# Epsilon as a third triple of the variance, and a reordered first chunk, in a fused attention and gated-unit kernel

## The chip, the cores and the metric

The kernel runs on one core of a Trainium2 chip. The metric is device time in microseconds, the median over several executions. In the traces the core's engines are PE (TensorE; PEld is its weight loads), DVE (VectorE), ACT (ScalarE), POOL (GpSimd) and SP (SyncE, which here only issues DMAs). All times below are microseconds unless marked otherwise, and "L193" is line 193 of the kernel before the change.

## What is computed

Two branches read the same layer-normed input and are added to the input itself:

```python
xn = layernorm(x, eps=1e-5)                      # x: 2048 rows of 512, bf16
# A: attention, 32 heads of 16, each row sees itself and the 255 rows before it
q, k, v = split(xn @ wqkv)                       # wqkv: 512 x 1536
p = softmax(mask(q k^T / 4, window 256))
a = (p v) @ wo                                   # wo: 512 x 512
# B: bilinear gated unit
b = ((xn @ w_gate) * (xn @ w_up)) @ w_down       # 512 x 1792, 512 x 1792, 1792 x 512
out = x + a + b
```

The layer norm has neither scale nor shift: each row is `(x - mean) * (var + 1e-5) ** -0.5`.

## The kernel before

The 2048 rows are cut into 16 blocks of 128 rows, and four blocks make a chunk T of 512 rows, so there are four chunks. All weights are loaded once, by DMAs that SP issues at the start: x of blocks 0, 1 and 2 to 3 first, then the three thirds of Wqkv (V, K, Q), then halves of the gate and up weights, the rest of x and the other weights.

The order of instructions on every engine is written out by hand. `run` walks through a list of attention steps and, between them, takes pieces of other matrix work (projections of the next chunk, gate, up and down products) from the list that `fillers` makes, by a running count of PE time; each engine then executes its own instructions in that order and waits on semaphores for the others. `copy` picks ACT or DVE for an eviction by booked time, unless the caller names the engine. `PADS` puts 298 empty PE instructions (nops, L682) into two later stretches.

What matters here is how a block is normed, and the start.

For block t, `norm_stats` (L187) runs two DVE instructions: `bn_stats` (L193) turns the 512 values of a row into two triples of count, mean and sum of squares (6 numbers), and `bn_aggr` (L194) joins the triples into a mean and a variance (`mv`). `norm_scale` (L198) adds 1e-5 to the variance (`ve`, L203: on DVE for block 0, on POOL for all others) and takes the power -0.5 on POOL (`rs`, L206). `norm_apply` (L210) writes `xn = (x - mean) * rs` on DVE (L214). The tile `xn` has two buffers. `norm_transpose` (L219) turns a block by four PE transposes into a bank of PSUM (`xTp`, L233), which ACT copies to `xnT` (L234); from chunk 1 on, a DMA does this instead (L227).

PSUM has eight banks. Four of them ("M" banks) are taken in turn by `m_tile`; the other four make the score tile S, which the first attention step fills. `usual_banks(3)` starts the turn at bank 3.

The start goes like this on PE. `setup` first writes a zero tile and calls `keep_busy(40)`: 40 matmuls of 128 columns on that tile (`wps`, L151), whose result nobody reads. Then `first_chunk` (L292) follows. On DVE it puts the stats of blocks 0 and 1, then xn of block 0, the stats of block 2, xn of block 1, the stats of block 3, and xn of block 2. On PE it puts the transposes of block 0, `keep_busy(8)`, and then, for each block b from 0 to 3, the transposes of block b + 1 followed by the four matmuls of V of block b (`proj_v`, `vp`, L263). The copy of a V block from PSUM (L256 on DVE, L254 on ACT for block 2) is issued right behind its matmuls, and xn of block 3 is issued on DVE behind the copy of V0:

```python
for b in range(4):
    if b < 3:
        self.norm_transpose(b + 1, False)
    self.proj_v(b, engine="act" if b == 2 else "dve")
    if b == 0:
        self.norm_apply(3)
```

The K and Q projections of the chunk (`qkp`, L275) come next, and then the attention steps with their fillers. The norms of later chunks run among the fillers, in the same functions.

Of the kernel before, what the change touches and what calls it, by code (L numbers as in the profile page):

```python
# [8 lines left out]
F32 = mybir.dt.float32  # L9
I32 = mybir.dt.int32  # L10
ACT = mybir.ActivationFunctionType
ALU = mybir.AluOpType
# [24 lines left out]
class Kernel:  # L37
    def __init__(self, ctx, tc, x, wqkv, wo, wg, wu, wd, out):
        self.ctx, self.tc, self.nc = ctx, tc, tc.nc
        _, S, D = x.shape  # L40
        self.S, self.D, self.F = S, D, wg.shape[1]
        assert D == 512 and S % 512 == 0 and self.F % 256 == 0
        self.NT, self.NCH, self.NF = S // 128, S // 512, self.F // 128
        self.x_d, self.out_d = x.flatten_outer_dims(), out.flatten_outer_dims()
        self.w_d = dict(qkv=wqkv, o=wo, g=wg, u=wu, d=wd)

        def pool(name, bufs, **kw):
            return ctx.enter_context(tc.tile_pool(name=name, bufs=bufs, **kw))

        self.const = pool("const", 1)  # L50
        self.chunk2 = pool("chunk2", 2)
        self.qpool = pool("qpool", 5)
        self.kpool = pool("kpool", 9)
        self.hpool = pool("hpool", self.NF + FIRST)
        self.ppool = pool("ppool", 11)
        self.work = pool("work", 2)
        self.small = pool("small", 4)
        self.work1 = pool("work1", 1)
        self.psum = []
        self.usual_banks(3)  # L60

    def open_banks(self, name, bufs=1):

# [18 lines left out]
    def setup(self):  # L82
        nc, const, NT, NF = self.nc, self.const, self.NT, self.NF
        self.x = const.tile([128, NT, 512], BF16, name="x")
        self.Wqkv = const.tile([128, 4, 1536], BF16, name="Wqkv")
        self.Wo = const.tile([128, 4, 512], BF16, name="Wo")
        self.Wg = const.tile([128, 4, self.F], BF16, name="Wg")
        self.Wu = const.tile([128, 4, self.F], BF16, name="Wu")
        self.Wd = const.tile([128, NF, 512], BF16, name="Wd")
        xv = self.x_d.rearrange("(t p) d -> p t d", p=128)  # L90
        wq = self.w_d["qkv"].rearrange("(k p) n -> p k n", p=128)
        wg = self.w_d["g"].rearrange("(k p) n -> p k n", p=128)
        wu = self.w_d["u"].rearrange("(k p) n -> p k n", p=128)
        for lo, hi in ((0, 1), (1, 2), (2, 4)):
            nc.sync.dma_start(out=self.x[:, lo:hi, :], in_=xv[:, lo:hi, :])
        for lo in (1024, 512, 0):
            nc.sync.dma_start(out=self.Wqkv[:, :, lo:lo + 512], in_=wq[:, :, lo:lo + 512])
        h = self.F // 2
        for lo in (0, h):
            nc.sync.dma_start(out=self.Wg[:, :, lo:lo + h], in_=wg[:, :, lo:lo + h])  # L100
            nc.sync.dma_start(out=self.Wu[:, :, lo:lo + h], in_=wu[:, :, lo:lo + h])
            if lo == 0:
                nc.sync.dma_start(out=self.x[:, 4:8, :], in_=xv[:, 4:8, :])
        nc.sync.dma_start(out=self.Wd[:], in_=self.w_d["d"].rearrange("(f p) n -> p f n", p=128))
        wo = self.w_d["o"].rearrange("(c p) n -> p c n", p=128)
        for c in range(4):
            nc.sync.dma_start(out=self.Wo[:, c, :], in_=wo[:, c, :])
        for lo, hi in ((8, 10), (10, 12), (12, NT)):
            nc.sync.dma_start(out=self.x[:, lo:hi, :], in_=xv[:, lo:hi, :])

        self.idle = const.tile([128, 128], BF16, name="idle")
        nc.vector.memset(self.idle[:], 0.0)
        self.keep_busy(40)
        warm = const.tile([128, 1], F32, name="warm")
        nc.vector.memset(warm[:], 0.0)
        nc.scalar.activation(out=warm[:], in_=warm[:], func=ACT.Exp)
        ident = const.tile([128, 128], BF16, name="ident")
        nc.gpsimd.memset(ident[:], 0.0)
        nc.gpsimd.affine_select(out=ident[:], in_=ident[:], compare_op=ALU.not_equal, fill=1.0,
                                base=0, pattern=[[-1, 128]], channel_multiplier=1)  # L120
        self.ident = ident
        pi = const.tile([128, 1], I32, name="pi")
        nc.gpsimd.iota(pi[:], pattern=[[0, 1]], base=0, channel_multiplier=1)
        podd = const.tile([128, 1], I32, name="podd")
        nc.vector.tensor_scalar(out=podd[:], in0=pi[:], scalar1=4, scalar2=1,
                                op0=ALU.arith_shift_right, op1=ALU.bitwise_and)
        self.odd = const.tile([128, 1], F32, name="odd")
        nc.vector.tensor_copy(out=self.odd[:], in_=podd[:])
        self.even = const.tile([128, 1], F32, name="even")
        nc.vector.tensor_scalar(out=self.even[:], in0=self.odd[:], scalar1=-1.0, scalar2=1.0,  # L130
                                op0=ALU.mult, op1=ALU.add)
        self.mhalf = const.tile([128, 4], F32, name="mhalf")
        nc.gpsimd.memset(self.mhalf[:], -0.5)
        self.diag = const.tile([128, 64], BF16, name="diag")
        self.far = const.tile([128, 64], BF16, name="far")
        nc.gpsimd.memset(self.diag[:], BIG)
        nc.gpsimd.memset(self.far[:], BIG)
        for half in (slice(0, 64), slice(64, 128)):
            self.triangle(self.diag[half], True)
            self.triangle(self.far[half], False)  # L140
        self.xnT, self.Q, self.hT, self.OT = {}, {}, {}, {}
        self.K, self.V, self.VS = {}, {}, {}
        self.strips, self.parts, self.at = {}, {}, {}
        self.stock = []
        self.new_values()
# [41 lines left out]
    def norm_stats(self, t, n=4):  # L187

        nc = self.nc
        if t % n == 0:  # L190
            self.mv = self.small.tile([128, n, 2], F32, tag="mv", name="mv")
        st = self.small.tile([128, 6], F32, tag="st")
        nc.vector.bn_stats(out=st[:], in_=self.x[:, t, :])  # L193
        nc.vector.bn_aggr(out=self.mv[:, t % n, :], in_=st[:])  # L194
        self.book("dve", STATS)
        self.stats[t] = [self.mv, t % n, None]

    def norm_scale(self, t, n=4):  # L198

        nc = self.nc  # L200
        mv = self.stats[t][0]
        ve = self.small.tile([128, n], F32, tag="ve", name="ve")
        (nc.gpsimd if t else nc.vector).tensor_scalar(out=ve[:], in0=mv[:, :, 1], scalar1=1e-5, scalar2=None,  # L203
                                                      op0=ALU.add)
        rs = self.small.tile([128, n], F32, tag="rs", name="rs")
        nc.gpsimd.tensor_tensor(out=rs[:], in0=ve[:], in1=self.mhalf[:, 0:n], op=ALU.pow)  # L206
        for u in range(t, t + n):
            self.stats[u][2] = rs

# [45 lines left out]
        else:  # L255
            nc.vector.tensor_copy(out=out, in_=in_)  # L256

    def proj_v(self, t, ks=range(4), engine=None):
        nc = self.nc
        T, b = divmod(t, 4)  # L260
        ps = self.bank(ks, "vp")
        for k in ks:
            nc.tensor.matmul(ps[:], lhsT=self.xnT[T][:, b, k, :],  # L263
                             rhs=self.Wqkv[:, k, 1024:1536], start=(k == 0), stop=(k == 3))
        if 3 not in ks:
            return
        self.copy(self.heads(self.V[T])[:, b].rearrange("p (r g) d -> p r g d", r=2)[:, :, :, 0:16],
                  ps.rearrange("p (g r d) -> p r g d", g=16, r=2), engine)
# [23 lines left out]
    def first_chunk(self):  # L292

        self.new_chunk(0)
        for b in range(2):
            self.norm_stats(b, 1)
            self.norm_scale(b, 1)
        for b in (0, 1, 2):
            self.norm_apply(b)
            if b < 2:  # L300
                self.norm_stats(b + 2, 1)
                self.norm_scale(b + 2, 1)
        self.norm_transpose(0, False)
        self.keep_busy(8)
        for b in range(4):
            if b < 3:
                self.norm_transpose(b + 1, False)
            self.proj_v(b, engine="act" if b == 2 else "dve")
            if b == 0:
                self.norm_apply(3)  # L310
        self.proj_qk(0, 0, 1, engine="dve")
        self.proj_qk(0, 0, 0, engine="act")
        self.swap_halves(0, self.nc.scalar)
        self.proj_qk(0, 1, 1, engine="dve")
# [491 lines left out]
```

## Time and profile before

| | |
|---|---|
| median of 3 runs | 262.12 (262.10 to 262.45) |
| the profiled execution's own time | 262.46 |
| its span, from first to last instruction | 260.6 |
| instructions with a duration | 7774 |
| DMA traffic | 9.70 MB read, 2.10 MB written |

The span is what the profile's views cover; 1.86 of the profiled run lies around it. The profile's busy time of PE counts matmuls whose ends are modelled, so a busy PE may still have waited; only starts are measured. The granted clock of TensorE is 1.00 in every slice of the page. The most numerous group on POOL is the masking of attention probabilities (L182, 224 instructions, 98.7 busy), and on ACT the exponentials (L353, 66 of one form, 123.8 busy). The DMA engines are full from about 2 to 32, while the weights arrive.

In a line of the timeline, the columns are start, time from the first start to the last end, engine, line, operation, output and inputs, shapes and the number of instructions that the line merges; in brackets stands how long the engine had been idle before and what ended that.

### The profile page before, as it was taken

Reading aid. Unit: us, or ns where it says so; the run is one execution under the profiler, and the core shown is the slowest. Engines: PE = TensorE matmul, PEld = TensorE weight load, DVE = VectorE, ACT = ScalarE, POOL = GpSimd, SP = SyncE. Lnnn points to the kernel's source line nnn. Section 1 sums busy time; section 2 is a strip of 40 time slices with the busy share of each in tenths; the row PEclk is TensorE's granted clock in tenths of the full one; section 3 lists DMA queues with packets and bytes.
Section 4 is the critical chain, followed back from the end, with each engine's and each line's share of the span. In section 5 each row is a group of like instructions: output and inputs, shape, how many; then the busy total and the mean of one; then the engine's idle time right before and its main releaser. Section 6 shows DMA issues by size and latency. Waiting matters only on the chain.

```text
span 260.6 us, 7774 instructions
## 1 busy us (share of the span) xinstructions
PE 256.4 (98%) x3170; PEld 120.1 (46%) x3170; DVE 169.0 (65%) x342; ACT 183.4 (70%) x167; POOL 114.7 (44%) x278
## 2 busy tenths in 40 slices
PE   8999999999999999999999999999999999999995
PEld 8444444444444544444544454444544445444453
DVE  6687898888836487347976468642895235948144
ACT  3377788888586788787756768879874877877500
POOL 6216242425356745343445764334242565543500
DMA  6999910120013220002001301000200100000002
GB/s 207 377 353 336 283 27 20 24 48 1 3 40 43 60 25 1 3 0 48 3 3 41 82 24 23 0 4 1 48 5 4 36 23 24 3 0 3 3 0 83
DMA packets 19426, 15.04 MB, mean 58 GB/s; under 512 B 7360, under 2 KB 19392, under 8 KB 19392
## 3 DMA queue, kind: packets, MB, share of 16 engines
q1 hardware_dynamic: 18848, 14.26, 19.7%
q8 instruction: 26, 0.43, 0.7%
q10 hardware_dynamic: 544, 0.30, 0.4%
q14 instruction: 8, 0.07, 0.1%
HBM read 9.70 MB, written 2.10 MB: 45 GB/s over the span
## 4 chain that ended last, share of the span: by engine, by line
PE 91%; DVE 7%; issue 1%
PE up L513 17%; PE gp L502 17%; PE psd L535 16%; PE qkp L275 10%; PE S L350 8%; PE acc L473 6%; PE vp L263 6%; PE psd L541 5%; PE L L535 2%; PE wps L151 2%; DVE at L479 2%; DVE hT L518 1%; DVE on L492 1%; PE B L350 1%; PE L L541 1%
## 5 line engine op out<-in xcount | busy, mean ns | idle before, releaser
L182 POOL TENSOR_SCALAR_AFFINE_SELECT P<-P 64x256 bf16<-64x256 bf16 x224 | 98.7, 441 | 122.4 <-ACT P L353 110.7
L353 ACT ACTIVATE P<-S 128x2048 bf16<-128x2048 f32 x66 | 123.8, 1876 | 23.3 <-PE S L350 22.4
L502 PE MATMUL gp<-xnT,Wg 128*128 128x512 bf16 x224 | 59.1, 380 | 0.0
L513 PE MATMUL up<-xnT,Wu 128*128 128x512 bf16 x224 | 59.0, 380 | 0.0
L518 DVE TENSOR_TENSOR hT<-up,gsb 128x512 bf16<-128x512 f32 x56 | 38.0, 683 | 24.7 <-ACT gsb L254 12.7
L535 PE MATMUL psd<-Wd,hT 128*128 128x512 bf16 (+1 forms) x210 | 47.8, 369 | 0.0
L448 DVE TENSOR_TENSOR P<-P,diag 128x512 bf16<-128x512 bf16 (+1 forms) x75 | 30.1, 401 | 16.0 <-ACT P L353 15.9
L254 ACT ACTIVATE gsb<-gp 128x512 bf16<-128x512 f32 x49 | 28.5, 596 | 9.5 <-PE gp L502 9.4
L535 PEld LDWEIGHTS <-hT 128*128 128x128 bf16 x238 | 21.6, 98 | 25.5 <-issue 3.1
L513 PEld LDWEIGHTS <-Wu 128*128 128x128 bf16 x224 | 20.6, 98 | 25.6 <-issue 2.7
L502 PEld LDWEIGHTS <-Wg 128*128 128x128 bf16 x224 | 20.5, 98 | 25.5 <-issue 2.9
L353 ACT ACTIVATE P<-B 128x1536 bf16<-128x1536 f32 (+2 forms) x18 | 17.8, 1022 | 17.7 <-PE B L350 10.8
L275 PE MATMUL qkp<-xnT,Wqkv 128*128 128x512 bf16 x128 | 29.8, 380 | 0.0
L350 PE MATMUL S<-Q,K 32*128 32x320 bf16 (+4 forms) x624 | 28.7, 255 | 0.0
L350 PEld LDWEIGHTS <-K 32*128 32x128 bf16 x720 | 11.4, 92 | 27.4 <-issue 26.5
L551 DVE TENSOR_TENSOR x<-psd,x 128x512 bf16<-128x512 f32 (+1 forms) x15 | 9.9, 665 | 20.8 <-PE psd L541 20.8
L479 DVE STREAM_TRANSPOSE at<-acc 128x512 f32<-128x512 f32 x30 | 19.1, 688 | 4.6 <-PE acc L473 4.6
L275 PEld LDWEIGHTS <-Wqkv 128*128 128x128 bf16 x128 | 11.8, 98 | 14.7 <-issue 1.6
L473 PE MATMUL acc<-P,VS 64*32 64x320 bf16 (+4 forms) x672 | 17.6, 253 | 0.0
L473 PE MATMUL acc<-P,V 64*32 64x320 bf16 (+4 forms) x672 | 17.2, 253 | 0.0
L473 PEld LDWEIGHTS <-VS 64*32 64x32 bf16 x720 | 15.4, 91 | 2.2 <-issue 1.5
L263 PE MATMUL vp<-Wqkv,xnT 128*128 128x512 bf16 x64 | 15.3, 380 | 0.0
(56 smaller groups left out, 191.3 us busy)
## 6 DMA issues: line engine op xcount, KB each, us to landing
out_dram<-x SPq DMA_DIRECT2D x15, 128.0 KB, 1.7
Wg<-in_B_w_gate_dram SPq DMA_DIRECT2D x2, 896.0 KB, 11.3
Wu<-in_B_w_up_dram SPq DMA_DIRECT2D x2, 896.0 KB, 12.4
Wd<-in_B_w_down_dram SPq DMA_DIRECT2D x1, 1792.0 KB, 16.7
Wqkv<-in_A_wqkv_dram SPq DMA_DIRECT2D x3, 512.0 KB, 6.3
x<-in_A_x_dram SPq DMA_DIRECT2D x2, 512.0 KB, 8.8
VS<-V SPq DMA_DIRECT2D x6, 144.0 KB, 2.6
x<-in_A_x_dram SPq DMA_DIRECT2D x3, 256.0 KB, 6.7
```

Source lines behind the costliest of these rows:

```text
L182: nc.gpsimd.affine_select(out=v, in_=v, pattern=pattern + [[1 if diag else -1, 64]], compare_op=ALU.is_ge if diag else ALU.is_gt, fill=0.0 ...
L254: nc.scalar.activation(out=out, in_=in_, func=ACT.Copy)
L263: nc.tensor.matmul(ps[:], lhsT=self.xnT[T][:, b, k, :], rhs=self.Wqkv[:, k, 1024:1536], start=(k == 0), stop=(k == 3))
L275: nc.tensor.matmul(ps[:], lhsT=self.Wqkv[:, k, lo:lo + 128], rhs=self.xnT[T][:, :, k, :], start=(k == 0), stop=(k == 3))
L350: self.nc.tensor.matmul(kw.pop("out"), start=True, stop=True, skip_group_check=True, **kw)
L353: self.nc.scalar.activation(out=out, in_=in_, func=ACT.Exp, scale=0.25)
L448: self.nc.vector.tensor_tensor(out=v, in0=v, op=ALU.min, in1=self.diag.unsqueeze(1).unsqueeze(1).to_broadcast([128, 4, n, 64]))
L473: nc.tensor.matmul(accs[par][32 * e:32 * e + 32, q:q + n], lhsT=v, rhs=P[rows, e, col:col + n], start=(i == 0), stop=(i == len(todo) - 1), ...
L502: nc.tensor.matmul(ps[:], lhsT=self.Wg[:, k, 128 * f:128 * f + 128], rhs=self.xnT[T][:, :, k, :], start=(k == 0), stop=(k == 3))
L513: nc.tensor.matmul(ps[:], lhsT=self.Wu[:, k, 128 * f:128 * f + 128], rhs=self.xnT[T][:, :, k, :], start=(k == 0), stop=(k == 3))
L518: nc.vector.tensor_tensor(out=self.hT[T, f][:], in0=ps[:], in1=self.gsb[:], op=ALU.mult)
L535: nc.tensor.matmul(ps, lhsT=self.hT[T, f][:, 128 * b:128 * b + 128], rhs=self.Wd[:, f, c0:c1], start=(f == 0), stop=False)
```

## The change

There are five edits.

1. The statistics of a block go to a slice of a fixed tile `st` of 4 x 9 values instead of a fresh one of 6. The last three values of each slice are written once, by two POOL memsets in `setup`: count 0, mean 0, and a sum of squares of 512e-5. `bn_aggr` reads all nine, so that the variance comes out with 1e-5 in it. The addition `ve` is gone for all 16 blocks, and the power reads the variance directly.
2. The idle matmuls are 36 and 6 instead of 40 and 8.
3. xn of block 3 is issued on DVE ahead of V0's copy instead of behind it.
4. V0 is summed in the first bank of the score tile S instead of in an M bank. The turn of the M banks starts at 0 instead of 3, so that with one tile fewer taken from it every later tile has the bank that it had.
5. 4, 4 and 5 nops follow the matmuls of V1, V2 and V3 on PE.

```diff
-        self.usual_banks(3)
+        self.usual_banks(0)
...
-        self.keep_busy(40)
+        self.keep_busy(36)
...
+        self.st = const.tile([128, 4, 9], F32, name="st")
+        nc.gpsimd.memset(self.st[:, :, 6:8], 0.0)
+        nc.gpsimd.memset(self.st[:, :, 8:9], 512 * 1e-5)
         self.mhalf = const.tile([128, 4], F32, name="mhalf")
...
-        st = self.small.tile([128, 6], F32, tag="st")
-        nc.vector.bn_stats(out=st[:], in_=self.x[:, t, :])
-        nc.vector.bn_aggr(out=self.mv[:, t % n, :], in_=st[:])
+        st = self.st[:, t % 4, :]
+        nc.vector.bn_stats(out=st[:, 0:6], in_=self.x[:, t, :])
+        nc.vector.bn_aggr(out=self.mv[:, t % n, :], in_=st)
...
-        ve = self.small.tile([128, n], F32, tag="ve", name="ve")
-        (nc.gpsimd if t else nc.vector).tensor_scalar(out=ve[:], in0=mv[:, :, 1], scalar1=1e-5, scalar2=None,
-                                                      op0=ALU.add)
         rs = self.small.tile([128, n], F32, tag="rs", name="rs")
-        nc.gpsimd.tensor_tensor(out=rs[:], in0=ve[:], in1=self.mhalf[:, 0:n], op=ALU.pow)
+        nc.gpsimd.tensor_tensor(out=rs[:], in0=mv[:, :, 1], in1=self.mhalf[:, 0:n], op=ALU.pow)
...
-    def proj_v(self, t, ks=range(4), engine=None):
+    def proj_v(self, t, ks=range(4), engine=None, ps=None):
...
-        ps = self.bank(ks, "vp")
+        if ps is None:
+            ps = self.bank(ks, "vp")
...
         self.norm_transpose(0, False)
-        self.keep_busy(8)
+        self.keep_busy(6)
+        self.norm_apply(3)
+        S = self.s_tiles.tile([128, 4, 512], F32, tag="S", name="S")
         for b in range(4):
             if b < 3:
                 self.norm_transpose(b + 1, False)
-            self.proj_v(b, engine="act" if b == 2 else "dve")
-            if b == 0:
-                self.norm_apply(3)
+            self.proj_v(b, engine="act" if b == 2 else "dve", ps=None if b else S[:, 0, :])
+            for _ in range((0, 4, 4, 5)[b]):
+                self.nc.tensor.nop("pad", nofuse=True)
```

## The prediction

> **What bounds the kernel now.** I read the page first, then the timeline from 3 to 14 us engine by engine, because the diff acts there, and last every place where TensorE (PE) stands still. On the page:
>
> ```profile
> PE 256.4 (98%) x3170; PEld 120.1 (46%) x3170; DVE 169.0 (65%) x342; ACT 183.4 (70%) x167; POOL 114.7 (44%) x278
> ...
> PE 91%; DVE 7%; issue 1%
> ```
>
> The chain that ended last is PE nearly throughout, and POOL and ACT are not in it. So time can only come from PE being given less to do or from PE standing still less. PE's timeline at the start:
>
> ```profile
> 5.30 0.62 PE L233 MATMUL xTp<-ident,xn 128*128 128x128 bf16 x4
> 5.71 1.06 PE L151 MATMUL wps<-idle 128*128 128x128 bf16 x8
> 6.56 0.59 PE L233 MATMUL xTp<-ident,xn 128*128 128x128 bf16 x4
> 6.98 1.03 PE L263 MATMUL vp<-Wqkv,xnT 128*128 128x512 bf16 x4
> 7.85 0.39 PE L233 MATMUL xTp<-ident,xn 128*128 128x128 bf16 x4
> 8.07 1.03 PE L263 MATMUL vp<-Wqkv,xnT 128*128 128x512 bf16 x4
> 9.12 0.40 PE L233 MATMUL xTp<-ident,xn 128*128 128x128 bf16 x4
> ```
>
> Only the starts are used here, since the ends are modelled. Two things are to be seen. First, PE's pace doubles: eight idle matmuls take 6.56 - 5.71 = 0.85, 0.107 each; the four transposes of block 1 take 6.98 - 6.56 = 0.42, 0.105 each; but the four of block 2 take 8.07 - 7.85 = 0.22, 0.055 each, and the four 512-column matmuls of V0 take 0.87, 0.216 each. The doubling falls at about 6.98 (the granted clock reads 1.00 on both sides, so it must be read from spacings). Second, V1's four matmuls from 8.07 need 0.86 and are done at 8.93, but the next transpose starts at 9.12: PE stands still for 0.19. The wait is on the weight loads, in PEld's timeline, and DVE's timeline tells why:
>
> ```profile
> 9.11 0.23 PEld L233 LDWEIGHTS <-xn 128*128 128x128 bf16 x4 [0.51 <-DVE xn L214]
> ```
>
> ```profile
> 3.03 0.69 DVE L193 BATCH_NORM_STATS2 st<-x 128x6 f32<-128x512 bf16 x1 [1.01 <-DMA x<-in_A_x_dram]
> 3.75 0.18 DVE L194 BATCH_NORM_AGGREGATE mv<-st 128x2 f32<-128x6 f32 x1
> 3.97 0.15 DVE L203 TENSOR_SCALAR ve<-mv 128x1 f32<-128x1 f32 x1
> 4.04 0.68 DVE L193 BATCH_NORM_STATS2 st<-x 128x6 f32<-128x512 bf16 x1
> 4.76 0.18 DVE L194 BATCH_NORM_AGGREGATE mv<-st 128x2 f32<-128x6 f32 x1
> 4.86 0.38 DVE L214 TENSOR_SCALAR xn<-x,mv,rs 128x512 bf16<-128x512 bf16 x1
> 5.16 0.68 DVE L193 BATCH_NORM_STATS2 st<-x 128x6 f32<-128x512 bf16 x1
> 5.87 0.18 DVE L194 BATCH_NORM_AGGREGATE mv<-st 128x2 f32<-128x6 f32 x1
> 6.01 0.41 DVE L214 TENSOR_SCALAR xn<-x,mv,rs 128x512 bf16<-128x512 bf16 x1
> 6.34 0.69 DVE L193 BATCH_NORM_STATS2 st<-x 128x6 f32<-128x512 bf16 x1
> 7.06 0.18 DVE L194 BATCH_NORM_AGGREGATE mv<-st 128x2 f32<-128x6 f32 x1
> 7.19 0.41 DVE L214 TENSOR_SCALAR xn<-x,mv,rs 128x512 bf16<-128x512 bf16 x1
> 8.05 0.69 DVE L256 CAST V<-vp 128x512 bf16<-128x512 f32 x1 [0.45 <-PE vp L263]
> 8.65 0.41 DVE L214 TENSOR_SCALAR xn<-x,mv,rs 128x512 bf16<-128x512 bf16 x1
> ```
>
> Block 3's xn stands behind V0's copy (8.05). Block 0's xn ends at 5.24 and PE takes it at 5.30, just as the 40 idle matmuls run out. From 9.4 on, no gap between matmul starts is over 0.1 longer than the work between them, but for 0.28 at 133.8 and at 196.9, both behind DVE. So the rest should move as one block.
>
> **The change, part by part.** Handovers read off these rows: DVE to POOL 0.09 (4.94 to 5.03), POOL to DVE 0.04 (rs of block 1 ends 5.97, xn 6.01), DVE to PE 0.05, the next DVE instruction 0.08 before the end of the last (5.24 to 5.16), aggregate 0.03 behind its stats. POOL's pow rows are 0.55 to 0.57.
>
> *Epsilon.* Removed: one ve on DVE (3.97) and 15 on POOL (0.22 to 0.36). Added: two POOL memsets near 1.4 (rows of 0.10; the aggregate that waits for them starts at 3.75, and POOL's other memsets, which they push back, end at 3.03 now, a microsecond before its first pow) and three more values in each aggregate. No row has 9 values: below, nothing (a larger input gives no reason for a gain); above, one more whole aggregate, 0.18. One-value DVE operations take 0.15 and the 6-value aggregate 0.18, so three more values lie nearest to 0.01; I take 0. Then: aggregate 0 ends 3.93, pow 4.02 to 4.57; stats 1 from 3.85 (x has landed: issued by 1.7, at most 2.9 to landing), aggregate 1 at 4.56 to 4.74; xn0 when DVE is free, 4.66 to 5.04 (pow alone would allow 4.61). Block 1: stats 4.96 to 5.64, aggregate to 5.85, pow 4.83 to 5.40, xn1 5.77 to 6.18. Block 2: xn2 6.92 to 7.33. Block 3: aggregate ends 7.00, pow 7.09 to 7.66. The 12 later ve on POOL are worth nothing: POOL is not in the chain.
>
> *Idle matmuls.* Six times 0.107 = 0.64 leaves PE, but it pays only as far as data is there. The 36 end at 4.87; xn0 reaches PE at 5.09, so PE stands still for 0.22. Transposes 5.09 to 5.52, six idle to 6.16, xn1 reaches PE at 6.23: block 1's transposes start 0.33 earlier than 6.56, and V0's sum at 6.66 instead of 6.98. Its weights are there (first Wqkv issue 2.2 + 4.1 = 6.3). If the pace still doubles at 6.98, V0 has 0.32 at half pace (a 512-column matmul at half pace, four times 0.107 = 0.43, is 0.75 done), then 0.05 and 3 x 0.216: it ends 7.68 instead of 7.85. Half of the lead goes there; 0.17 stays.
>
> *Block 3 first.* xn3 starts at 7.70 (pow 7.66), ends 8.11 and reaches PE at 8.16. PE, with block 2's transposes 7.68 to 7.90 and V1 to 8.76, takes it at 8.77: the stall of 0.19 is gone with 0.6 to spare. The step issues no DMA, and the order on the queues of SP and ACT stays. Queued behind it on DVE is V0's copy, 8.03 to 8.72 against 8.05 to 8.74 now; V1's copy needs V1's sum at about 8.95. Nobody is late. Start of block 3's transposes: 8.77 against 9.12, a gain of 0.35 = 0.17 + 0.18.
>
> *Score bank.* V0's sum leaves bank 0, which V2's sum takes at 9.00. V0's copy would have freed it at 8.72, so this is worth nothing, and costs nothing: the first score matmul is at 13.76. All later bank turns are the same.
>
> *Nops.* 13 nops come; 12 instructions of the idle matmuls and a separate wait of PE before V0 go, so PE's later instructions keep their places. The 298 nops that there are (L682) take 0.013 each, and among them four 512-column matmuls still take 0.87 (107.09 to 107.96). Hidden behind 0.86 of queued matmuls I count 0; uncovered, 13 x 0.013 = 0.17.
>
> V2 then starts 9.00, V3 when ACT has copied block 3 (9.20 to 9.80 plus 0.05) at 9.86, as closely as now. Sum: 0.35. The profiled execution is 260.6 in a run of 262.46, so 1.86 lies around the span; it would be 260.25 and 262.11. The three runs' median is 262.12, 0.34 under the profiled one; the forecast from it is 261.77. The gain hardly depends on where the pace doubles: worked through with the doubling at 5.5 or at 7.5 in both kernels, it comes out near 0.35 again, since in the old kernel V0's copy, and so xn3, moves along with it (at 5.5: new, xn1 at 6.23, xn2 at 7.38, block 3 at 8.46; old, xn2 at 7.65, V0's sum ready at 7.76, xn3 at 8.78, block 3 at 8.83).
>
> **Rivals.** *The doubling comes late (slower).* PE now has holes of 0.22 and 0.07 before 6.98, where before it had none of over 0.02 from 1.04 on. For: the doubling came 5.94 after the first idle matmul, with PE never still. Against: both holes together are 5% of that. If the long hole restarts the count, it comes at 5.09 + 5.94 = 11.03. From 6.66, 16 V matmuls and 8 transposes are 7.69 at half pace and 3.90 at full; 4.37 of them go at half pace (57%), the rest takes 1.68, so projections start at 12.71 instead of 11.08: 1.63 lost, 263.75. Each microsecond of delay costs 0.5, so it decides from a doubling 0.7 late, at 7.68, where the gain of 0.35 is eaten up. The Trainium skill (TensorE: Matmul & The Clock Gate, "Part 1: The HAM clock gate") has a reason for this rival: activity is judged over free-running windows of about 3.4 us, and full rate needs a busy one; "Part 4: PE-mode transpose" adds that transposes do not count as busy in the same way. By one window more, 10.39, an estimate from that page gives 1.32 lost, 263.4. This trace, with 0.107 before and 0.055 after, agrees that there are two paces, but cannot show what a hole does.
>
> *More than forecast.* If x lands 0.3 earlier than here, the old kernel stays held by its idle matmuls and V0's copy, while the new one starts V0 at 6.37 and gains 0.51; at most all six idle matmuls come back, 0.64. So 261.5 to 261.6. For: xn0 and the end of the idle run coincide to 0.02, so an earlier x would be hidden before. Against: nothing shows x landing earlier.
>
> *The aggregate doubles.* At 0.18 more each, xn1 stands behind three of them and xn2 behind four: xn1 reaches PE at 6.23 + 0.54 = 6.77, V0's sum starts by 7.20 at the latest (6.77 + 0.43) and is done in 0.86, before xn2 is there: xn2 reaches PE at 7.33 + 0.72 + 0.05 = 8.10. V1 then runs 8.32 to 9.19, and block 3's transposes start there, 0.07 later than now: 262.2. So even a doubled aggregate costs the whole gain and hardly more, since the stall before block 3 is still removed.
>
> *A later wait takes it back.* The two 0.28 waits behind DVE, or the weights arriving until about 28: the first gate weights land near 15 and are used at 18.9, so little speaks for it: 262.1.
>
> **Numbers.** Forecast 0.50, more 0.22, aggregate 0.07, later wait 0.03, late doubling 0.18. 0.2% is 0.52, about what a measurement of this kernel can tell from no change. The runs spread by 0.35, so of the forecast case I count 0.12 as over 0.52 faster and 0.38 as same; of the second 0.16 and 0.06; aggregate and later wait are same: faster 0.28, same 0.54, slower 0.18. The range, 261.35 to 262.45, is the forecast with that spread, the second rival and the two without gain; the late doubling is left out.
>
> **What would show it.** Right: no ve rows; xn0 at about 4.66, xn3 ahead of the first V copy; aggregates of 0.18 to 0.20; transposes at about 5.09, 6.23, 7.7 and 8.8; the first 512-column projection (L276) at 10.73. Wrong: transposes of block 2 at 0.107 each; L276 after 11.1; a longer aggregate; a gain at 11 that is gone at 130.

## The result and the profile after

The changed kernel takes 261.55 (median of 21 runs, 261.31 to 262.75) against 262.33 for the kernel before, measured beside it (21 runs). The ratio is 0.9972, with a 95% interval of 0.9963 to 0.9981: 0.73 faster, and the interval leaves 0.50 to 0.97. The profiled run took 261.67 with a span of 259.9, against 262.46 and 260.6. The forecast was 261.77, a gain of 0.35 on a kernel before at 262.12.

The page of the changed kernel: the same engine is busy, and POOL has 13 instructions fewer.

```profile
PE 255.9 (98%) x3164; PEld 119.5 (46%) x3164; DVE 168.4 (65%) x341; ACT 183.4 (71%) x167; POOL 110.9 (43%) x265
...
PE 91%; DVE 7%; issue 1%
```

PE's timeline at the start (columns as before; in this kernel the idle matmuls are L154, V's matmuls L264, the projections of K and Q L276):

```profile
5.04 0.61 PE L233 MATMUL xTp<-ident,xn 128*128 128x128 bf16 x4
5.44 0.85 PE L154 MATMUL wps<-idle 128*128 128x128 bf16 x6
6.16 0.60 PE L233 MATMUL xTp<-ident,xn 128*128 128x128 bf16 x4
6.71 1.02 PE L264 MATMUL S<-Wqkv,xnT 128*128 128x512 bf16 x4
7.57 0.39 PE L233 MATMUL xTp<-ident,xn 128*128 128x128 bf16 x4
7.79 1.03 PE L264 MATMUL vp<-Wqkv,xnT 128*128 128x512 bf16 x4
8.66 0.39 PE L233 MATMUL xTp<-ident,xn 128*128 128x128 bf16 x4
8.88 1.89 PE L264 MATMUL vp<-Wqkv,xnT 128*128 128x512 bf16 x8
10.61 0.59 PE L276 MATMUL qkp<-xnT,Wqkv 128*128 128x512 bf16 x2
```

The transposes of blocks 0 to 3 start at 5.04, 6.16, 7.57 and 8.66; the prediction had 5.09, 6.23, 7.68 and 8.77. V1's four matmuls from 7.79 need 0.86 and end at 8.65, and block 3's transposes start at 8.66: the stall of 0.19 is gone. The first projection (L276) starts at 10.61; 10.73 was forecast, 11.08 was the start before. DVE's timeline:

```profile
3.70 0.20 DVE L197 BATCH_NORM_AGGREGATE mv<-st 128x2 f32<-128x9 f32 x1
3.82 0.65 DVE L196 BATCH_NORM_STATS2 st<-x 128x6 f32<-128x512 bf16 x1
4.50 0.20 DVE L197 BATCH_NORM_AGGREGATE mv<-st 128x2 f32<-128x9 f32 x1
4.61 0.37 DVE L214 TENSOR_SCALAR xn<-x,mv,rs 128x512 bf16<-128x512 bf16 x1
...
5.73 0.37 DVE L214 TENSOR_SCALAR xn<-x,mv,rs 128x512 bf16<-128x512 bf16 x1
...
7.68 0.41 DVE L214 TENSOR_SCALAR xn<-x,mv,rs 128x512 bf16<-128x512 bf16 x1 [0.44 <-POOL rs L206]
8.01 0.69 DVE L256 CAST V<-S 128x512 bf16<-128x512 f32 x1
```

The aggregate of nine values takes 0.196 against 0.182 for six. The ve rows are gone, and block 3's xn (7.68) stands ahead of V0's copy (8.01). Up to the last matmul the lead of 0.47 at the first projection holds but for 0.04: it starts at 257.01 against 257.44. Two single executions are compared here. x of block 0 landed at 2.88 in this one and at 3.00 in that of the kernel before, and V's weights at 6.67 and 6.32, so not all of the 0.47 need be the work of the edits.

The rest of the gain lies behind the last matmul. DVE's last row under the span, first of the kernel before and then of the changed one:

```profile
core 0 of [0], span 260.6 us
...
257.69 0.29 DVE L551 TENSOR_TENSOR x<-psd,x 128x128 bf16<-128x128 f32 x1 [0.45 <-PE psd L541]
```

```profile
core 0 of [0], span 259.9 us
...
257.27 0.29 DVE L554 TENSOR_TENSOR x<-psd,x 128x128 bf16<-128x128 f32 x1 [0.45 <-PE psd L544]
```

From the end of that row to the end of the span it was 260.61 - 257.98 = 2.63, and is now 259.87 - 257.56 = 2.31. The trace names the place: the last thing on the core is a hand-shake in which the engines wait for POOL, and POOL's last step in it, between two semaphore instructions (the timeline view leaves these out), takes 0.370 before (260.13 to 260.50) and 0.079 after. That is 0.29. So by the two traces the gain of 0.74 is 0.43 of an earlier start and 0.29 of a shorter end, and the rest lies between the last matmul and POOL's step.

### The profile page after: what moved, and what is told of

It is laid out like the page before. It is cut to its first block, busy times and chain, and to the rows that moved or that the text cites. A ratio compares the mean times of both kernels' runs of the same rounds, so it can differ in the third digit from the quotient of the medians.

```text
span 259.9 us, 7760 instructions
## 1 busy us (share of the span) xinstructions
PE 255.9 (98%) x3164; PEld 119.5 (46%) x3164; DVE 168.4 (65%) x341; ACT 183.4 (71%) x167; POOL 110.9 (43%) x265
## 4 chain that ended last, share of the span: by engine, by line
PE 91%; DVE 7%; issue 1%
PE up L516 17%; PE gp L505 17%; PE psd L538 16%; PE qkp L276 10%; PE S L353 8%; PE acc L476 6%; PE vp L264 5%; PE psd L544 5%; PE L L538 2%; DVE at L482 2%; PE wps L154 2%; DVE hT L521 1%; DVE on L495 1%; PE B L353 1%; PE L L544 1%
## 5 line engine op out<-in xcount | busy, mean ns | idle before, releaser
L276 PE MATMUL qkp<-xnT,Wqkv 128*128 128x512 bf16 x128 | 29.8, 380 | 0.0
L276 PEld LDWEIGHTS <-Wqkv 128*128 128x128 bf16 x128 | 11.8, 98 | 14.7 <-issue 1.6
L544 PE MATMUL psd<-Wo,OT 128*128 128x512 bf16 (+1 forms) x60 | 14.9, 369 | 0.0
```

The lines of the kernel that those rows point to most:

```text
L276: nc.tensor.matmul(ps[:], lhsT=self.Wqkv[:, k, lo:lo + 128], rhs=self.xnT[T][:, :, k, :], start=(k == 0), stop=(k == 3))
L544: self.nc.tensor.matmul(ps, lhsT=self.OT[T][:, c, 128 * b:128 * b + 128], rhs=self.Wo[:, c, c0:c1], start=False, stop=(c == 3))
```

## Experiments

Two theories stood. The end theory: the time at the end is given by the length of POOL's program, whatever the 13 instructions do. The start theory, its rival: all of the gain is the path to the first projection, as forecast. For the later runs a second question was whether at the start V0 waits for the landing of its weights, so that the idle matmuls matter little. The ratios below are to the kernel before on the same chip, and 0.001 is 0.26; the intervals are some 0.25 to 0.4 either way, so that a term of 0.2 is read from the traces.

**Epsilon alone, and everything but epsilon.** The first is the kernel before with only edit 1; the second is the changed kernel with the old `st`, `ve` and `rs`.

```diff
 only_epsilon       = before + edit 1
 without_epsilon    = after  - edit 1
```

> The kernel before with the epsilon edit alone (third triple, no ve). Two theories for the measured gain of 0.7, of which the two traces show 0.43 to 0.47 in the first chunk and 0.29 in the last barrier, where POOL's step from 260.13 to 260.50 takes 0.37 before and 0.08 after. Start theory: the whole gain is made in the first chunk, and the barrier's difference is chance: PE is still held by 40 idle matmuls and by V0's copy ahead of block 3, so this kernel is 0 to 0.15 faster than before. End theory: about 0.3 comes from POOL's program being 13 instructions shorter (283 to 270), so that the end no longer crosses into a new 8 KB block of instructions: this kernel, with 270, is 0.3 to 0.45 faster, and its last barrier step takes 0.08.

> The changed kernel with the epsilon edit taken back (ve is there again, POOL has 283 instructions), all else as changed. Start theory: xn of block 1 reaches PE 0.2 later, block 3 is still ahead of V0's copy, so most of the gain stays: 0.4 to 0.6 faster than before. End theory: only the start's part stays, 0.2 to 0.3, and the last barrier step takes 0.37 again.

Measured: 262.09, ratio 0.9988 (0.9978 to 0.9997), and 262.20, ratio 0.9996 (0.9988 to 1.0005). POOL's last step is 0.078 in the first and 0.370 in the second, as the end theory had it. The start theory's 0.4 to 0.6 for without_epsilon lies outside the interval (-0.13 to 0.31); the times of only_epsilon fit both theories.

**POOL's program by itself.** One kernel gives the changed one 13 POOL instructions that nobody needs, ahead of the end of the program; the other takes 13 memsets off POOL in the kernel before and gives them to DVE.

```diff
 pool_padded (after)
+        for _ in range(13):
+            self.nc.gpsimd.memset(self.mhalf[:], -0.5)
         self.close_banks(5)
 before_trimmed (before), 13 memsets of setup and new_values
-        nc.gpsimd.memset(...)
+        nc.vector.memset(...)
```

> The changed kernel with 13 memsets of a constant tile added at the end of POOL's program, where POOL is idle: 283 instructions again. Start theory: as the changed kernel, 0.7 faster than before. End theory: 0.4 to 0.45 faster, the last barrier step takes 0.37 and one more 8 KB instruction block is fetched.

> The kernel before with its 13 memsets moved from POOL to DVE, so POOL has 270 instructions; nothing else is changed. Start theory: no change, within 0.1. End theory: 0.3 faster, the last barrier step takes 0.08.

Measured: 262.02, ratio 0.9993 (0.9982 to 1.0003), and 262.05, ratio 0.9987 (0.9977 to 0.9998). POOL's last step is 0.370 with the padding and 0.079 in the trimmed kernel. From the start of the last matmul to the end of the span it is 3.14 to 3.17 in the four kernels with 278 POOL instructions (the kernel before, without_epsilon, pool_padded and only_order below), and 2.85 to 2.87 in the ten with 265; POOL's last step is 0.370 in all four and 0.078 or 0.079 in all ten. (The expectations count 283 and 270, the traces 278 and 265 with a duration; the difference of 13 is the same.) Trimming alone is worth 0.34 by the median ratio (interval 0.05 to 0.60) and epsilon alone 0.31 (0.08 to 0.58), which fits that epsilon alone pays through POOL's program. The end theory's POOL step held in both kernels. Of its times, the 0.3 of the trimmed kernel held; the padded one was only 0.18 faster (-0.08 to 0.47) where 0.4 to 0.45 was expected, at the upper edge of that interval; the start theory's 0.7 is outside it. The profiled execution of the padded kernel had one more stall, 0.46 of PE at 93.4, so its span of 260.8 is not used.

What makes the step long stays open. Shown is that the number of POOL's instructions decides, and only these two lengths were run. The trace has fetches of instruction blocks, and in a queue of 8,192-byte fetches there are nine from the start of the span in the long kernels, the last near 261, and eight in the short ones, the last at 215 to 224. So POOL's program may cross one more block at its very end. The Trainium skill (Runtime: NRT & Kernel Launch, "Instruction fetch mechanics") says that a crossing of a block is mostly hidden, and gives blocks of 16 KiB. Here the fetches of this queue are of half that size, and those of another queue are of 16,384 bytes. But POOL did not wait for the ninth block to land: in all four long kernels this fetch starts 0.6 to 0.9 after the end of the span, and POOL's last instruction is over by then. That issuing it takes the 0.29 is not shown.

**Order, idle matmuls, nops.** Each takes one edit back from the changed kernel.

```diff
 order_back
-        self.norm_apply(3)
...
+            if b == 0:
+                self.norm_apply(3)
 idle_back
-        self.keep_busy(36)
+        self.keep_busy(40)
...
-        self.keep_busy(6)
+        self.keep_busy(8)
...
-            for _ in range((0, 4, 4, 5)[b]):
+            for _ in range((0, 0, 0, 1)[b]):
 no_nops
-            for _ in range((0, 4, 4, 5)[b]):
+            for _ in range((0, 0, 0, 0)[b]):
```

> The changed kernel with xn of block 3 behind V0's copy again, all else as changed. The first four runs put 0.29 of the gain into POOL's shorter program; that stays here. If the 0.19 that PE stood still before block 3's transposes is a term of its own, it comes back: 0.45 to 0.55 faster than before, and PE takes block 3 about 0.2 later than in the changed kernel. If V0's earlier copy has swallowed that stall anyway: 0.7 faster, as the changed kernel.

> The changed kernel with 40 and 8 idle matmuls (and one nop instead of 13, so that PE has as many instructions as before), all else as changed. If the fewer idle matmuls are a term of their own: block 1's transposes at 6.5 again instead of 6.2, half of it lost where the pace is doubled late: 0.45 to 0.6 faster than before. If V0 waits for its weights (they landed at 6.67 in the changed kernel's trace) and not for PE: 0.7 faster, as the changed kernel.

> The changed kernel without its 13 nops, so that all later PE instructions stand 13 places earlier. If places do not matter: as the changed kernel, 261.55 (the nops themselves are hidden). If the places decide when PE fetches its blocks of instructions against its other work: a stall like the one of 0.46 at 93.4 in the trace of pool_padded appears or moves, and the median is 0.2 to 0.5 above the changed kernel.

Measured: 261.66, ratio 0.9963 (0.9948 to 0.9978); 261.54, ratio 0.9959 (0.9943 to 0.9975); 261.52, ratio 0.996 (0.9946 to 0.9975). None is told apart from the changed kernel by its time: the three ratios lie below its 0.9972, but the intervals overlap, the kernel before was itself at 262.57 on that chip, and the medians alone are 261.66, 261.54 and 261.52 against 261.55. So for edits 2, 3 and 5 no worth of their own is shown in time; edit 4 was not taken back by itself. The traces do tell the order apart. From V0's first matmul to the first projection it takes 4.09 with xn3 behind V0's copy (before, only_epsilon, before_trimmed and order_back alike) and 3.90 to 3.95 with xn3 ahead of it (after, its repeat, idle_back, no_nops): the step is worth 0.14 to 0.19. In pool_padded, with xn3 ahead too, it takes 4.01; there the pace doubled only at 6.98, 0.21 behind V0's start. DVE's rows in order_back show the old order, in which xn3 comes 0.45 later than in the changed kernel:

```profile
7.52 0.69 DVE L256 CAST V<-S 128x512 bf16<-128x512 f32 x1 [0.24 <-PE S L264]
8.13 0.40 DVE L214 TENSOR_SCALAR xn<-x,mv,rs 128x512 bf16<-128x512 bf16 x1
```

The idle matmuls and V0's weights are read from this table of single profiled executions. "Stats" is the start of block 0's stats, which follows the landing of x; "weights" is the landing of V's third of Wqkv, by its semaphore.

| kernel | stats | T0 after stats | T1 after stats | weights | V0 | V0 to first projection |
|---|---|---|---|---|---|---|
| before | 3.03 | 2.27 | 3.53 | 6.32 | 6.98 | 4.09 |
| after | 2.90 | 2.14 | 3.26 | 6.67 | 6.71 | 3.90 |
| after, again | 2.92 | 2.15 | 3.27 | 6.32 | 6.42 | 3.95 |
| only_epsilon | 2.93 | 2.36 | 3.56 | 6.70 | 6.83 | 4.09 |
| without_epsilon | 3.01 | 2.27 | 3.46 | 6.69 | 6.73 | 4.05 |
| order_back | 2.94 | 2.15 | 3.27 | 6.42 | 6.46 | 4.09 |
| idle_back | 2.97 | 2.15 | 3.27 | 6.46 | 6.50 | 3.92 |
| no_nops | 2.94 | 2.14 | 3.26 | 7.54 | 7.58 | 3.90 |

Three things are in it. Epsilon brings T0 0.13 and T1 0.20 closer to the stats (without_epsilon against after). The idle matmuls hold T0 by 0.22 where the pace is still halved (only_epsilon, 2.36 against 2.14), and by nothing where it has doubled early (idle_back, doubled at 4.85). And V0 starts 0.04 behind the landing of its weights in after, without_epsilon, order_back, idle_back and no_nops: there the weights are the last to come, and whatever T1 gained is lost. They landed between 6.32 and 7.54, though all these kernels issue the same transfers.

**The order alone.** The kernel before with edit 3 and nothing else.

```diff
 only_order (before)
+        self.norm_apply(3)
         for b in range(4):
...
-            if b == 0:
-                self.norm_apply(3)
```

> The kernel before with block 3 scaled ahead of V0's copy and nothing else: V0's sum stays in its bank, the idle matmuls, epsilon and POOL's program too. Theory one (this step is worth 0.18 by itself, and needs no score bank): block 3's transposes start when V1 ends, without the stall of 0.19, projections of Q and K 0.15 to 0.2 earlier than in the kernel before, POOL's last step still 0.37; 0.1 to 0.2 faster. Rival (the copy of V0, now behind xn3, gives its bank back late): V2 starts later and the gain is gone, within 0.05 of the kernel before.

Measured: 262.52 against 262.24, ratio 1.001 (1.0 to 1.0019): not faster, and more likely slower (by 0.26, interval 0.00 to 0.50). Theory one fell; the rival's mechanism held, and it cost rather more than the 0.05 that it allowed. The views of POOL, DVE and PE in that kernel, in this order:

```profile
7.25 0.35 POOL L203 TENSOR_SCALAR ve<-mv 128x1 f32<-128x1 f32 x1 [0.18 <-DVE mv L194]
7.68 0.57 POOL L206 TENSOR_TENSOR rs<-ve,mhalf 128x1 f32<-128x1 f32 x1
```

```profile
8.29 0.41 DVE L214 TENSOR_SCALAR xn<-x,mv,rs 128x512 bf16<-128x512 bf16 x1 [0.76 <-POOL rs L206]
8.61 1.28 DVE L256 CAST V<-vp 128x512 bf16<-128x512 f32 x2
```

```profile
8.76 0.40 PE L233 MATMUL xTp<-ident,xn 128*128 128x128 bf16 x4
9.35 1.89 PE L263 MATMUL vp<-Wqkv,xnT 128*128 128x512 bf16 x8 [0.20 <-DVE V L256]
```

With `ve` still on POOL, rs of block 3 ends at 8.25, where in the changed kernel it ends at 7.65 (its row there is `7.02 0.63 POOL L206`). So xn3 starts 0.6 later, V0's copy behind it starts at 8.61, and V2, which needs the bank that this copy empties, waits for it until 9.35; its transposes were issued from 8.76 and take 0.22, so it is 0.37 late. From V0 to the first projection it takes 4.44. So by these rows edit 3 pays in full only where edit 1 shortens POOL's part and edit 4 takes V0 out of that bank. In without_epsilon, which has edits 3 and 4 but not 1, the same stretch is 4.05.

**Late doubling of PE's pace.** 12 idle matmuls ahead of block 0 in place of 36, first as it is, then with 48 nops that keep the places of all later PE instructions.

```diff
 few_idle
-        self.keep_busy(36)
+        self.keep_busy(12)
 few_idle_padded
-        self.keep_busy(36)
+        self.keep_busy(12)
+        for _ in range(48):
+            nc.tensor.nop("pad", nofuse=True)
```

> The changed kernel with 12 idle matmuls at the start instead of 36, so PE stands still from about 2.3 to 5.0. If a hole in PE's work puts off the doubling of its pace (the prediction's slower rival): the doubling comes at 8.5 to 12, transposes of block 2 at 0.107 each, and 0.9 to 2.6 slower than the changed kernel, 262.4 to 264.2. If the doubling is set by time alone: at 4.4 to 7 as in the runs so far, and 261.5, no change to the changed kernel.

> The changed kernel with 12 idle matmuls ahead of block 0 instead of 36, and 48 PE nops behind them, so that all later instructions of PE keep their places. Theory one (of the 7.2 that 12 idle matmuls cost, 2.0 is the late doubling of PE's pace and the rest comes from the moved places of PE's instructions): the doubling again at 10 to 11, projections of Q and K at 12.4 to 12.7, and no stall of PE of 0.9 or more behind that: 1.9 to 2.2 slower than the changed kernel, 263.4 to 263.9. Rival (the cold start brings the later stalls too): 268 to 269, with the stalls and the half pace near 195 again.

Measured: 268.75, ratio 1.0218 (1.0193 to 1.0244), and 263.20 (262.35 to 264.4), ratio 1.0035 (1.0019 to 1.0051). In the profile the padded kernel doubles its pace at 10.27 and reaches the first projection at 12.35, 1.74 to 1.98 later than the two profiles of the changed kernel. By medians it is 1.73 slower than the changed kernel beside it (261.47), and its runs spread by 2.05. So the late doubling is real; the rival's 1.63, for a doubling at 11.03 and counted from the kernel before, is of that size. few_idle itself is some 7 slower than the changed kernel. The other 5 of that are something else, which no theory had. The first line below is from few_idle's waits (engine, line, what it waited for: us in total, times, longest); the others are from its windows (length, then busy time and count of PE, PEld, DVE, ACT, POOL, granted clock, DMA share, GB/s):

```profile
PE acc L476 <- issue: 4.6, 4, 1.8
```

```profile
191.74:195.15 3.41, 1.58 (x97) 0.93 (x78) 1.56 (x3) 0.71 (x1) 1.64 (x4) 1.00 0.02 5
195.15:198.56 3.41, 3.41 (x9) 1.19 (x10) 2.52 (x6) 1.88 (x1) 0.89 (x2) 0.50 0.00 0
```

Four times PE stands still in the midst of the attention matmuls with nothing to wait for (1.6, 1.0, 2.1 and 0.9 from one start to the next), and after the third the granted clock halves for 3.41. The profiled execution is the slowest of the six (270.8), and its last matmul is 9.1 later than the changed kernel's: 2.0 of that lie ahead of the first projection, and we estimate 5.5 for the four gaps and 1.7 for the stretch at half pace. With the 48 nops there is no such stall.

The trace points to what PE waited for. In the queue of 16,384-byte instruction fetches a fetch ends at 126.39, 156.92, 192.56 and 224.57, and PE goes on at 127.85, 158.38, 193.98 and 225.93, that is 1.36 to 1.46 later each time. The stall of 0.46 in pool_padded fits too: the fetch ends at 92.66, and PE goes on at 94.08. So PE very likely ran out of instructions, at places that moved with the number of instructions ahead; no run varied the fetches by themselves. no_nops, 13 places off, showed no such stall. Why these places and not others stays open.

**V's weights earlier.** The changed kernel with V's third of Wqkv issued by ACT's queue at 0.81, while SP issues the rest.

```diff
 wv_early
-        for lo in (1024, 512, 0):
+        nc.scalar.dma_start(out=self.Wqkv[:, :, 1024:1536], in_=wq[:, :, 1024:1536])
+        for lo in (512, 0):
```

> The changed kernel with V's third of Wqkv issued by ACT's queue ahead of its first activation, instead of as the fourth transfer on SP's queue. Theory one (V0 is held by the landing of these weights, so that neither fewer idle matmuls nor an earlier xn1 can pay): they land by about 5, V0 starts as soon as T1 is copied, at 6.35 to 6.55 instead of 6.7, and the run is 0.15 to 0.3 faster than the changed kernel. Rival: the transfers share what they can move, x(2:4) lands later than 5.1 and xn2 is late in its place: V0 earlier, but the projections of Q and K at 10.5 to 10.6 as before, and no faster.

> The changed kernel unaltered, for comparison with the other three on one chip. Our theory: 0.7 to 0.9 under the kernel before; 0.29 of that in POOL's last step, the rest in the first chunk.

Measured: 264.35, ratio 1.0077 (1.0064 to 1.009), while the changed kernel beside it took 261.47, ratio 0.997 (0.9958 to 0.9981). Both theories of wv_early fell: it is 2.9 slower. The landings (KB each, then us from issue to landing), DVE's, PE's and the windows' lines:

```profile
Wqkv<-in_A_wqkv_dram ACTq DMA_DIRECT2D x1, 512.0 KB, 4.2
...
x<-in_A_x_dram SPq DMA_DIRECT2D x1, 256.0 KB, 4.4
```

```profile
5.38 0.69 DVE L197 BATCH_NORM_STATS2 st<-x 128x6 f32<-128x512 bf16 x1 [1.39 <-DMA x<-in_A_x_dram]
```

```profile
6.65 0.40 PE L234 MATMUL xTp<-ident,xn 128*128 128x128 bf16 x4 [1.79 <-DVE xn L215]
...
7.77 0.51 PE L234 MATMUL xTp<-ident,xn 128*128 128x128 bf16 x4 [0.39 <-DVE xn L215]
```

```profile
4.50:7.91 3.41, 1.23 (x19) 0.89 (x17) 2.46 (x7) 0.66 (x2) 1.16 (x3) 1.00 1.10 358
7.92:11.33 3.41, 3.19 (x14) 1.65 (x14) 2.00 (x5) 1.19 (x2) 0.83 (x2) 0.50 1.07 375
```

The 512 KB on the second queue did land early, at 5.00 (issued at 0.81), as theory one had it. But x of block 1, 128 KB, landed at 5.36 instead of 3.3 to 3.4, and x of blocks 2 and 3 at 6.12: between 2.5 and 4.5 nearly all packets were those of the second queue. xn0, which stands behind block 1's stats on DVE, was late by 1.6, PE stood still, and the granted clock fell to half from 7.92 to 11.33. The rival had the sharing right, but not that V0 itself would be late: it starts at 8.08. The changed kernel's repeat shows what landing early is worth by itself: with its weights there at 6.32 (and the ratio within the 0.7 to 0.9 expected of it), V0 starts at 6.42 and the first projection at 10.37.

```profile
6.19 0.40 PE L233 MATMUL xTp<-ident,xn 128*128 128x128 bf16 x4
6.42 1.03 PE L264 MATMUL S<-Wqkv,xnT 128*128 128x512 bf16 x3
...
10.37 2.75 PE L276 MATMUL qkp<-xnT,Wqkv 128*128 128x512 bf16 x12
```

## Why the prediction came out as it did

The sign and the mechanism at the start were right; the sum was half of the gain, above all because one term was put at nothing. That 261.55 still lies within 261.35 to 262.45 is partly luck: this side of the range was there for an x that lands 0.3 earlier, and for the spread of the runs, not for the end of the program. To a gain of more than 0.52 the prediction gave a chance of 0.28.

- **Epsilon on DVE: right.** 0 was taken for three more values in the aggregate, between 0 and 0.18; it is 0.014. xn0 starts at 4.61 (4.66 forecast), xn1 reaches PE at 6.16 (6.23), xn3 starts at 7.68 (7.70). That these agree so closely is in part luck. x landed 0.12 earlier than in the profile before, and a cost was overlooked: in all ten kernels with the edit DVE has one more semaphore instruction ahead of its first aggregate, which then starts 0.11 behind its stats instead of 0.03. From the start of block 0's stats, xn0 comes 1.71 later, not 1.63. The rival of a doubled aggregate is out.
- **"The 12 later ve on POOL are worth nothing: POOL is not in the chain": the step that failed.** With the rest of the edit on POOL (15 ve go, two memsets come, 13 fewer in all) they are worth 0.29, at the end of the program and not where they stood. The chain as the profile draws it ends with DVE's last row, and the 2.6 behind it, where POOL is the last to arrive, were never priced.
- **Idle matmuls, 0.17: mis-sized, with two misses that offset each other.** "Its weights are there" was wrong in this execution: they landed at 6.67, not 6.3, and V0 started at 6.71 instead of 6.66. Against it, the pace doubled at 6.62 and not at 6.98, so that V0 lost nothing at half pace. V0 was done at 7.57 instead of 7.85, 0.28 earlier. What lets T1 start earlier was priced under this heading, but much of it is epsilon's: 0.20 at T1, while the idle matmuls hold PE only where the pace is still halved.
- **Block 3 first, 0.18: right in size (0.19), wrong as a step by itself.** The prediction held V0's copy harmless at 8.03 to 8.72, which presupposed epsilon's shorter POOL path. Without that and without the score bank the step loses what it gains (only_order).
- **"Score bank ... worth nothing, and costs nothing": not quite.** In the changed kernel's first profile V0's copy ends at 8.70 and V2 starts at 8.88, so an M bank would have done. In its repeat V2 starts at 8.64 and the copy ends at 8.71: there an M bank would have cost about 0.1, worked out from those rows and not run.
- **Nops, 0: right** as far as no_nops can tell (0.996 against 0.9972, overlapping intervals).
- **Sum at the first projection, 0.35: 0.47 seen**, and it moved on as one block but for 0.04, as forecast; the later wait is out. Around the span lay 1.86 before and 1.8 now.
- **Late doubling, 0.18: a real mechanism, which did not come about here.** The granted-clock records show what the prediction could not: the two half-pace stretches in the midst of a run (few_idle, wv_early) last 3.41 each, and the pace doubled at the end of a stretch of 3.41 in which PE was busy for 3.19 to 3.41 (from 4.4 to 7.0 in the kernels with 36 or 40 idle matmuls). It did not double after stretches with 2.52 or less (0.16 to 3.57 of pool_padded, 2.52; 3.45 to 6.86 of few_idle_padded, 1.80), and it fell back after 1.23 and 1.58. A hole does not restart a count at the hole's end, as the rival had it: in wv_early the pace changes at 4.50, 7.91 and 11.33, which are 3.41 apart, although the long hole ended at 6.65. Holes of 0.29 leave 3.12, for which no run here decides, and the changed kernel's two profiles had smaller holes. The Trainium skill (TensorE: Matmul & The Clock Gate, "Part 1: The HAM clock gate") has free-running windows of about 3.4, and the traces agree with it, with 3.41. Its table has the pace fall after an idle window; here windows in which PE was busy for 36% and 46% were enough.

What does not close: 0.73 less the end's 0.29 leaves 0.44 for the start, while pool_padded, which keeps the whole start and gives back the end, was only 0.18 faster than the kernel before (interval -0.08 to 0.47). Nor do the two halves add up: epsilon alone is worth 0.31 and the other four edits without it 0.10, together 0.41. What the edits are worth only together was not taken apart further. Those intervals overlap, and the landing of V's weights, which differs by up to 1.2 between executions, is of the same size.

## What to carry to other kernels

The end of the span has a chain of its own: before an instruction on an idle engine is priced at nothing, look at which engine arrives last in the closing steps, and how long its program is. An edit that shortens one path (block 3 ahead) may be worth only what another edit (epsilon, the bank) makes possible, so the rows behind the moved instruction have to be priced without the other edits too. And where a start waits for transfers, take the landing from several executions; moving a transfer to another queue can delay the small one that everything waits for.

## What was unexpected in the hardware

- 13 POOL instructions more or less, additions or memsets, decide between 0.370 and 0.079 for POOL's last step. Whether that goes against what the Trainium skill says of hidden crossings (Runtime: NRT & Kernel Launch, "Instruction fetch mechanics") is open, since the fetch that comes with it starts only after the span.
- PE can stand still amid short matmuls until 1.36 to 1.46 after an instruction fetch has ended, at places that depend on how many instructions stand ahead: 0.9 to 2.1 from start to start in few_idle, 0.46 lost once in pool_padded.
- A 512 KB transfer on a second queue, issued at 0.81, landed at 5.00 instead of 6.32 to 7.54, and delayed a 128 KB one on the first queue by 1.9 to 2.1 (5.36 against 3.27 to 3.44).
- Kernels with 36 or 40 idle matmuls have their pace double anywhere from 4.4 to 7.0 (6.62 and 5.76 in the two profiles of the changed kernel), and V's weights, issued in the same way, land anywhere from 6.32 to 7.54.
